# Low parts of w_out and w_in formed on GpSimd, with a new order of all steps, in an attention, SoLU and mixture-of-experts kernel

## The chip, the core and the metric

One NeuronCore of one Trainium2 chip runs the whole program. The metric is the device time of one execution in microseconds (us). Work is spread by hand over five engines: PE (TensorE, matmuls and transposes), DVE (VectorE), ACT (ScalarE), POOL (GpSimd) and SP (SyncE, which here issues most of the loads). Each engine carries out its own list of instructions strictly in order.

## The reference

Three layers, one after the other, on 4 batches of 768 tokens (3072 tokens of 320 values, 8 heads of 40):

```
# 1. gated linear attention, per batch and head, over time t
m_new = max(f[t] + m, i[t]);  f_stab = exp(f[t] + m - m_new);  i_stab = exp(i[t] - m_new)
C = f_stab * C + i_stab * v k^T;  n = f_stab * n + i_stab * k
y[t] = sigmoid(o_gate[t]) * (C q) / max(|n q|, 1)
# 2. SoLU layer: w_in is 320 x 1024, w_out is 1024 x 320
h = x @ w_in;  solu = h * softmax(h)
out = (layernorm(solu) * g_ln) @ w_out
# 3. experts: 8 of them, w1 320 x 1024, w2 1024 x 320, each token goes to one
logits = cosine(x, expert_emb) / tau;  e = argmax(logits)
out = softmax(logits)[e] * (relu(x @ w1[e]) @ w2[e])
```

## The kernel before

**Precision.** PE multiplies in a reduced format (fp32r). So that the result stays accurate, every large matrix is kept as a high part (the value cast to fp32r) and a low part (value minus high part, again fp32r), and a product is a sum of three: high by high, low by high, high by low. For w_in the parts are WH and WL, for w_out OH and OL.

**Attention.** The tokens are cut into 24 groups of 128, six per batch, handled side by side for the four batches' chunks. For each group there are the loads `load_q` (512 KB) and `load_n` (484 KB, keys, values and output gate), the scores S (PE, L626) weighted into Pt (DVE, L631), the values scaled by the gates (`scale_v`, POOL, L615; called vprep below), the numerator (PE, L637 and L642), the state (L647), and the denominator and gate (DVE, L654 to L662), which give X. X is transposed and split into xh and xl.

**SoLU layer.** `hidden` (L686 to L690) computes half of H = x @ w_in in one PSUM tile, and `hidden_pair` (L694, L695) ends it. There is one H tile: mm1 of group g+1 cannot begin before group g's H has been read for the last time. DVE takes the row maximum (L699, negmax), ACT the exponential (L704), DVE multiplies (L709, umul, the last reader of H). Then u is transposed, split, and multiplied with OH and OL (L748 to L750).

**Experts.** A routing stage runs every four or six groups (L783 to L845): POOL makes one-hot matrices ohr (L837) and ohv (L839), four pairs each time, which PE multiplies (L845, called invm). After the 24 groups, tokens are gathered per expert by indirect DMA (POOL, L1118), transposed on PE (L1129, xt), multiplied with the expert's weights, and scattered (L1222).

**The weights at the start.** w_in and w_out come as 64-bit floats. Each part is loaded by SP into a staging buffer `raw` (four slots, two per load, so a third load of this kind waits for the decode of the first), and DVE turns it into 32-bit values by three integer instructions (`decode`, L397 to L399; called dec_in0 to dec_in3 and dec_out0, dec_out1; the second and third instruction read two operands from SBUF). ACT casts the high parts (w_in: L421, called whi; w_out: L566, ohi). DVE forms the low parts: w_in by `in_lo` (L428, a subtract; called wlo(0) to wlo(3), 128x512 each) and w_out by `out_lo` (L569, one scale-and-subtract instruction; olo(0) to olo(7), 128x320 each). Half 0 of mm1 reads wlo(0) and wlo(2), half 1 reads wlo(1) and wlo(3). PE transposes w_out (L525, wtr), to fold the expert embedding in (L538, L546), and sums OH and OL over rows with eight matmul pairs (L576, cm).

**The gates.** A chain of its own: gate loads, a scan (L348), six matmuls (L356), a second scan (L358, gsum), twelve matmuls (L365), an exponential on ACT (L367, gives gw). vprep of the first group needs gw.

**What sets the order.** A table AT gives every step a number. The steps are sorted by it, and each engine's list is what results. The `after` and `war` arguments of `add` are used to make sure that the order is a legal one; waits in the program come from the data that an instruction reads and writes.

Of the kernel before, what the change touches and what calls it, by code (L numbers as in the profile page):

```python
# [9 lines left out]
F32 = mybir.dt.float32  # L10
# [48 lines left out]
BUFS = {"raw": 4, "qk": 4, "nat": 4, "Pt": 2, "X": 1, "xh": 2, "xl": 2, "e": 1, "u": 2, "ut": 1, "xg": 5, "yo": 3, "og": 1}  # L59
NFILL = 10  # L60
INP = ((0, 1), (1, 2), (2, 4), (4, 5))
# [157 lines left out]
def moe_kernel(ctx: ExitStack, tc: tile.TileContext, qkT, nat, gates, w_in, w_out, emb, w1, w2, cst, out):  # L219
# [59 lines left out]
    wts = {}  # L279
# [1290 lines left out]
```

## Time and profile before

| what | us |
|---|---|
| time, median of 3 runs | 524.79 (520.2 to 525.45) |
| the profiled execution's time | 522.23 |
| its span, first to last instruction | 520.4 |
| PE busy | 494.0 (95%) |
| DVE busy | 340.0 (65%) |
| ACT busy | 275.0 (53%) |
| POOL busy | 203.9 (39%) |

The profiled execution is one run; its own time is 2.6 us below the median. PE's share of busy time is an average: it is low in the first 48 us and at the end, and close to 100% in between. Times in the rows further below are us from the span's start.

### The profile page before, as it was taken

How to read it: one execution, taken by the hardware profiler on the slowest of the kernel's cores; microseconds unless marked ns; L12 is line 12 of the kernel's file. 1: busy time of each engine (PE TensorE's matmuls, PEld its weight loads, DVE VectorE, ACT ScalarE, POOL GpSimd, SP SyncE). 2: the span in 40 equal slices, each digit the busy share in tenths (PEclk: the TensorE clock that was granted, in tenths of full speed). 3: DMA queues.
4: the chain of work that ended last, by engine and by line, in shares of the span. 5: the costliest groups of instructions: out<-in, count | busy, mean ns of one | idle time of the engine just before them, and what ended most of it. 6: DMA issues, size and time to landing. Idle time of an engine off the chain costs nothing. (4 is left out here: it accounts for less than half of the span.)

```text
span 520.4 us, 14487 instructions
## 1 busy us (share of the span) xinstructions
PE 494.0 (95%) x5925; PEld 452.2 (87%) x5925; DVE 340.0 (65%) x735; ACT 275.0 (53%) x604; POOL 203.9 (39%) x350
## 2 busy tenths in 40 slices
PE   6869999999999999999999899999999999999991
PEld 5747998888899999889898789898999999999991
DVE  5997667777677587677778778677463655485120
ACT  3572555665656556666467565554543644565220
POOL 3221223266246247345315683656172444112021
PEclk9989999999999999999999899999999999999996
DMA  8962233343341253414041412835631861563000
GB/s 300 412 223 81 80 83 120 113 147 111 90 144 46 77 156 121 144 40 143 3 171 44 152 47 96 276 84 193 231 92 44 285 223 64 217 189 121 14 21 31
DMA packets 20139, 68.01 MB, mean 131 GB/s; under 512 B 2658, under 2 KB 6050, under 8 KB 19680
## 3 DMA queue, kind: packets, MB, share of 16 engines
q1 hardware_dynamic: 17120, 58.27, 33.5%
q0 software_dynamic: 2944, 8.73, 5.3%
q8 instruction: 49, 0.80, 0.7%
q14 instruction: 26, 0.21, 0.1%
HBM read 58.31 MB, written 8.72 MB: 129 GB/s over the span
## 5 line engine op out<-in xcount | busy, mean ns | idle before, releaser
L1222 POOL DMA_INDIRECT out_x<-you,sidx x28 | 30.8, 1099 | 95.5 <-ACT you L1215 82.9
L748 PE MATMUL Y<-OH,uh 128*128 128x328 f32 x192 | 63.4, 330 | 0.0
L1190 DVE SCALAR_TENSOR_TENSOR lu<-hpu,uu 128x384 fp32r<-128x384 f32 (+4 forms) x56 | 28.6, 519 | 53.0 <-ACT uu L1184 43.5
L750 PE MATMUL Y<-OH,ul 128*128 128x328 f32 x192 | 60.3, 314 | 0.2 <-DVE ul L740 0.2
L749 PE MATMUL Y<-OL,uh 128*128 128x328 f32 x192 | 60.4, 315 | 0.0
L1208 PE MATMUL ypu<-hr,uu 128*128 128x320 f32 (+4 forms) x192 | 60.1, 313 | 0.0
L1209 PE MATMUL ypu<-lr,uu 128*128 128x320 f32 (+4 forms) x192 | 59.3, 309 | 0.0
L1184 ACT ACTIVATE uu<-hpu 128x384 fp32r<-128x384 f32 (+7 forms) x64 | 30.4, 483 | 52.2 <-PE hpu L1161 40.0
L1109 DVE TENSOR_TENSOR lr<-raw,hr 128x1024 fp32r<-128x1024 f32 (+1 forms) x32 | 43.4, 1355 | 15.1 <-ACT hr L1102 15.1
L1210 PE MATMUL ypu<-hr,lu 128*128 128x320 f32 (+4 forms) x168 | 51.8, 309 | 0.0
L1102 ACT CAST hr<-raw 128x1024 fp32r<-128x1024 f32 (+1 forms) x40 | 45.2, 1134 | 10.5 <-DMA raw<-in_w 9.4
L736 ACT CAST uh<-tpu 128x512 fp32r<-128x512 f32 x48 | 27.7, 586 | 38.7 <-PE tpu L732 38.4
L704 ACT ACTIVATE e<-H,nmx 128x1024 f32<-128x1024 f32 x24 | 26.8, 1117 | 40.2 <-DVE nmx L699 40.2
L1118 POOL DMA_INDIRECT xgr<-ys,gidx x28 | 36.5, 1302 | 27.3 <-issue 8.9
L699 DVE TENSOR_REDUCE nmx<-H 128x1 f32<-128x1024 f32 x24 | 29.4, 1224 | 26.1 <-PE H L695 24.5
L1157 PE MATMUL hpu<-exr,hr 128*128 128x384 f32 (+7 forms) x128 | 43.7, 341 | 0.0
L1158 PE MATMUL hpu<-exr,lr 128*128 128x384 f32 (+7 forms) x128 | 42.5, 332 | 0.0
L1159 PE MATMUL hpu<-exr,hr 128*128 128x384 f32 (+7 forms) x128 | 42.4, 332 | 0.0
L686 PE MATMUL H<-WH,xh 128*128 128x512 f32 x96 | 40.7, 424 | 1.2 <-DVE u L709 1.1
L740 DVE TENSOR_TENSOR ul<-tpu,uh 128x512 fp32r<-128x512 f32 x48 | 32.4, 687 | 12.6 <-ACT uh L736 12.5
L687 PE MATMUL H<-WL,xh 128*128 128x512 f32 x96 | 37.9, 395 | 0.1
L748 PEld LDWEIGHTS Y<-OH,uh 128*128 128x128 f32 x192 | 36.2, 189 | 2.0 <-ACT yr L766 0.2
(230 smaller groups left out, 1351.3 us busy)
## 6 DMA issues: line engine op xcount, KB each, us to landing
qk<-in_qkT SPq DMA_DIRECT2D x24, 512.0 KB, 4.2
raw<-in_w SPq DMA_DIRECT2D x24, 512.0 KB, 4.7
nat<-in_nat SPq DMA_DIRECT2D x24, 484.0 KB, 3.7
raw<-in_w SPq DMA_DIRECT2D x16, 640.0 KB, 5.3
ys<-yr SPq DMA_DIRECT2D x5, 772.0 KB, 5.0
raw<-in_w_out SPq DMA_DIRECT2D x2, 1280.0 KB, 9.3
raw<-in_w_in SPq DMA_DIRECT2D x3, 512.0 KB, 6.4
raw<-in_w_in SPq DMA_DIRECT2D x1, 1024.0 KB, 8.3
```

Source lines behind the costliest of these rows:

```text
L686: T.matmul(out=o, lhsT=xh[:, kk, :], rhs=WH[:, kk, f], start=(kk == 0), stop=False)
L748: T.matmul(out=yp, lhsT=uh, rhs=OH[:, k, :], start=(k == 0), stop=False)
L749: T.matmul(out=yp, lhsT=uh, rhs=OL[:, k, :], start=False, stop=False)
L750: T.matmul(out=yp, lhsT=ul, rhs=OH[:, k, :], start=False, stop=(k == 7))
L1102: A.copy(out=R.h[i], in_=R.raw[i])
L1109: eng.tensor_tensor(out=R.l[i], in0=R.raw[i], in1=R.h[i].bitcast(F32), op=ALU.subtract)
L1157: T.matmul(out=o, lhsT=R.h[k][:, fs_], rhs=xh[:, k, tk], start=(k == 0), stop=False)
L1158: T.matmul(out=o, lhsT=R.l[k][:, fs_], rhs=xh[:, k, tk], start=False, stop=False)
L1159: T.matmul(out=o, lhsT=R.h[k][:, fs_], rhs=xl[:, k, tk], start=False, stop=False)
L1208: T.matmul(out=yp, lhsT=uh, rhs=hi, start=(f == 0), stop=False)
L1209: T.matmul(out=yp, lhsT=uh, rhs=lo, start=False, stop=False)
L1210: T.matmul(out=yp, lhsT=ul, rhs=hi, start=False, stop=(f == 7))
```

## The change

Four things change.

- The four low parts of w_in (wlo) are formed by POOL instead of DVE, with the same subtract.
- The eight low parts of w_out (olo) are formed by POOL. POOL's instruction is a plain subtract, so the scaling by g_ln is a new ACT instruction, `out_sc` (128x320, in place), one for each part; as it overwrites w_out's values, it stands behind the transposes wtr of the same part.
- The table AT has new numbers throughout. The loads and steps of the opening stand in another order, and so do steps on all engines later.
- PACE names, for eight expert weight loads, an earlier step that they are ordered behind.

```diff
+OLO_G, WLO_G, DEC_G = range(8), range(4), ()
+PACE = {(r, i): [("xc", u, 3)] for u, w in ((1, ((3, 1), (2, 3), (2, 2), (2, 1))), (3, ((3, 0), (4, 3), (3, 3), (3, 2)))) for r, i in w}
 AT = {
-    "f_in": "546 70 429 10",
+    "f_in": "498 167 373 2",
...
-            add(("wlo", j), "V", lambda j=j: in_lo(j, V), after=[("whi", j)])
+            add(("wlo", j), "G" if j in WLO_G else "V", lambda j=j: in_lo(j, G if j in WLO_G else V), after=[("whi", j)])
...
+    def out_sc(k):
+        A.mul(wts["o", k // 4][:, k % 4], wts["o", k // 4][:, k % 4], gl[:, k:k + 1])
+
     def out_lo(k):
-        V.scalar_tensor_tensor(out=wts["OL"][:, k, MAIN], in0=wts["o", k // 4][:, k % 4], scalar=gl[:, k:k + 1], in1=wts["OH"].bitcast(F32)[:, k, MAIN], op0=ALU.mult, op1=ALU.subtract)
+        if k in OLO_G:
+            G.tensor_tensor(out=wts["OL"][:, k, MAIN], in0=wts["o", k // 4][:, k % 4], in1=wts["OH"].bitcast(F32)[:, k, MAIN], op=ALU.subtract)
...
+        if k in OLO_G:
+            add(("osc", k), "A", lambda k=k: out_sc(k), after=[("ohi", k), ("wtr", k)])
+        add(("olo", k), "G" if k in OLO_G else "V", lambda k=k: out_lo(k), after=[("osc" if k in OLO_G else "ohi", k)])
...
-                add(("wl", r, i), "S", lambda r=r, R=R, i=i: w_load(R, od["ev", r], i), after=[("ev", r)], war=[("dec_out", 1)], take="raw", size=.512 * wsize(i))
+                add(("wl", r, i), "S", lambda r=r, R=R, i=i: w_load(R, od["ev", r], i), after=[("ev", r)] + PACE.get((r, i), []), war=[("dec_out", 1)], take="raw", size=.512 * wsize(i))
```

Line numbers after the change are 3 to 13 higher (L399 becomes L402, L428 becomes L431, L569 becomes L576 for POOL, L615 becomes L626, L699 becomes L710).

**First place: SP's first loads.** In the kernel before, SP's list begins with the constants cs and one part of w_in. raw is a load of w_in or w_out, 128x2560 is half of w_out.

```order
L313 DMA cs<-in_cst 128x329
L392 DMA raw<-in_w_in 128x1024
L312 DMA gx<-in_gates 32x768
L605 DMA qk_154<-in_qkT 128x1024
L311 DMA gt<-in_gates 32x1536
L612 DMA nat_158<-in_nat 128x968
L315 DMA cmb<-in_emb 8x320
L392 DMA raw<-in_w_in 128x1024
L605 DMA qk_169<-in_qkT 128x1024
L605 DMA qk_179<-in_qkT 128x1024
L392 DMA raw<-in_w_out 128x2560
```

The same place after the change, from the start of SP's list to the second part of w_in:

```order
L395 DMA raw<-in_w_in 128x1024
L395 DMA raw<-in_w_out 128x2560
L316 DMA cs<-in_cst 128x329
L623 DMA nat_154<-in_nat 128x968
L314 DMA gt<-in_gates 32x1536
L616 DMA qk_162<-in_qkT 128x1024
L623 DMA nat_164<-in_nat 128x968
L315 DMA gx<-in_gates 32x768
L318 DMA cmb<-in_emb 8x320
L395 DMA raw<-in_w_in 128x1024
```

Half of w_out moved from eleventh to second, and the constants and both gate loads (gt, gx) stand behind it.

**Second place: DVE from the last decodes to the first negmax.** Before, with wf a part of w_in, of a half of w_out, nmx the result of negmax(0):

```order
L399 SCALAR_TENSOR_TENSOR wf_210<-raw,wf_210 128x512
L428 TENSOR_TENSOR WL<-wf_511,WH 128x512
L428 TENSOR_TENSOR WL<-wf_210,WH 128x512
L428 TENSOR_TENSOR WL<-wf_511,WH 128x512
L560 TENSOR_TENSOR oe<-tpz,cs 128x64
L569 SCALAR_TENSOR_TENSOR OL<-of_256,cs,OH 128x320
L569 SCALAR_TENSOR_TENSOR OL<-of_386,cs,OH 128x320
L679 TENSOR_TENSOR xl_585<-tpx_558,xh_568 128x384
...
L569 SCALAR_TENSOR_TENSOR OL<-of_256,cs,OH 128x320
L569 SCALAR_TENSOR_TENSOR OL<-of_386,cs,OH 128x320
L699 TENSOR_REDUCE nmx_679<-H_161 128x1
```

After, on DVE, from X of the first group (X_362) to the last decode:

```order
L673 SCALAR_TENSOR_TENSOR X_362<-num_308,og_360 128x320
L642 TENSOR_TENSOR Pt_390<-S_1_342,cs 128x512
L642 TENSOR_TENSOR Pt_390<-S_1_343,cs 128x512
L400 TENSOR_SCALAR wf_416<-raw 128x1024
L401 SCALAR_TENSOR_TENSOR wf_416<-raw,wf_416 128x1024
L402 SCALAR_TENSOR_TENSOR wf_416<-raw,wf_416 128x1024
L400 TENSOR_SCALAR wf_213<-raw 128x512
L401 SCALAR_TENSOR_TENSOR wf_213<-raw,wf_213 128x512
L402 SCALAR_TENSOR_TENSOR wf_213<-raw,wf_213 128x512
```

The low parts are gone from DVE's list, and no decode of w_out is left behind X of the first group. And on POOL after the change, from its first low part to the last (nat is vprep; before, POOL's list holds only the rows of nat here):

```order
L431 TENSOR_TENSOR WL<-wf_213,WH 128x512
L576 TENSOR_TENSOR OL<-of_168,OH 128x320 x3
L626 TENSOR_TENSOR nat_154<-nat_154,gw 128x328
L626 TENSOR_TENSOR nat_184<-nat_184,gw 128x328
L576 TENSOR_TENSOR OL<-of_168,OH 128x320
L626 TENSOR_TENSOR nat_187<-nat_187,gw 128x328
L626 TENSOR_TENSOR nat_164<-nat_164,gw 128x328
L576 TENSOR_TENSOR OL<-of_266,OH 128x320 x2
L626 TENSOR_TENSOR nat_405<-nat_405,gw 128x328
L431 TENSOR_TENSOR WL<-wf_416,WH 128x512
L431 TENSOR_TENSOR WL<-wf_213,WH 128x512
L431 TENSOR_TENSOR WL<-wf_416,WH 128x512
```

Four low parts (wlo(1) and three olo) stand ahead of the first group's vprep, nat_154, and wlo(2), wlo(0), wlo(3) stand behind the fifth vprep.

**Third place: POOL at the fifth routing stage.** Before, with nmx21 the statistics of group 21 and ohr4, ohv4 the one-hot pairs:

```order
L715 TENSOR_SCALAR nmx21_4618<-nmx21_4618 128x1
L837 TENSOR_SCALAR ohr4_0_4693<-cs_75,vr4_4684 128x128
L839 TENSOR_SCALAR ohv4_0_4695<-cs_75,vr4_4684 128x192
L837 TENSOR_SCALAR ohr4_1_4723<-cs_75,vr4_4684 128x128
L839 TENSOR_SCALAR ohv4_1_4725<-cs_75,vr4_4684 128x192
```

And after:

```order
L848 TENSOR_SCALAR ohr4_2_4682<-cs_75,vr4_4663 128x128
L850 TENSOR_SCALAR ohv4_2_4684<-cs_75,vr4_4663 128x192
L848 TENSOR_SCALAR ohr4_3_4699<-cs_75,vr4_4663 128x128
L850 TENSOR_SCALAR ohv4_3_4701<-cs_75,vr4_4663 128x192
L724 TENSOR_SCALAR nmx21_4631<-nmx21_4631 128x1
```

Two of the four pairs moved ahead of the statistics of group 21. On DVE the key that they need (vr4) moved likewise, from behind umul(21) to ahead of the gating of group 23 and umul(21). PE's product of the pairs stands at the same place in both, between the two halves of mm2(21).

## Rows read from the trace of the kernel before

**Rows 1.** Waits of PE, whole span: what for, us in total, times, longest.
```profile
PE txr L1129 <- DMA xgr<-ys,gidx: 2.2, 3, 1.1
PE ip L845 <- POOL ohv L839: 1.9, 1, 1.9
PE H L686 <- DVE u L709: 1.1, 1, 1.1
```

**Rows 2.** Windows: us, busy PE PEld DVE ACT POOL, clock, DMA share, GB/s.
```profile
0.00:5.00 5.00, 1.83 (x8) 1.83 (x9) 1.68 (x5) 1.89 (x3) 3.10 (x17) 1.00 0.65 187
5.00:10.00 5.00, 4.07 (x32) 3.37 (x30) 2.99 (x4) 1.43 (x3) 0.00 (x0) 1.00 1.00 338
10.00:15.00 5.00, 4.85 (x28) 3.12 (x28) 4.39 (x9) 1.80 (x5) 0.83 (x2) 1.00 1.03 423
```

**Rows 3.** Timeline of PE, opening: start us, us, instruction, [idle before, releaser].
```profile
9.50 1.02 PE L356 MATMUL H<-gt,cs 128*128 128x512 f32 x2
...
38.45 0.48 PE L686 MATMUL H<-WH,xh 128*128 128x512 f32 x1
...
42.23 0.49 PE L694 MATMUL H<-WH,xl 64*128 64x512 f32 x1
...
48.10 0.47 PE L686 MATMUL H<-WH,xh 128*128 128x512 f32 x1 [1.06 <-DVE u L709]
```

**Rows 4.** Timeline of DVE, opening; columns as in the group before.
```profile
14.40 1.75 DVE L358 TENSOR_TENSOR_SCAN gx<-H,z 32x767 f32<-32x767 f32 x1 [0.48 <-PE H L600]
...
17.39 0.82 DVE L397 TENSOR_SCALAR of<-raw 128x1280 int32<-128x1280 int32 x1
...
19.77 1.91 DVE L399 SCALAR_TENSOR_TENSOR of<-raw,of 128x1280 int32<-128x1280 int32 x1
...
23.75 1.28 DVE L631 TENSOR_TENSOR Pt<-S,cs 128x512 f32<-128x512 f32 x2
...
31.50 1.17 DVE L397 TENSOR_SCALAR wf<-raw 128x1024 int32<-128x1024 int32 x1
...
35.38 0.43 DVE L397 TENSOR_SCALAR wf<-raw 128x512 int32<-128x512 int32 x1 [0.19 <-DMA raw<-in_w_in]
...
37.18 2.43 DVE L428 TENSOR_TENSOR WL<-wf,WH 128x512 fp32r<-128x512 f32 x3
...
39.67 1.00 DVE L569 SCALAR_TENSOR_TENSOR OL<-of,cs,OH 128x320 fp32r<-128x320 f32 x2
...
43.31 1.01 DVE L569 SCALAR_TENSOR_TENSOR OL<-of,cs,OH 128x320 fp32r<-128x320 f32 x2
44.23 1.22 DVE L699 TENSOR_REDUCE nmx<-H 128x1 f32<-128x1024 f32 x1
...
46.73 1.22 DVE L709 SCALAR_TENSOR_TENSOR u<-e,H 128x1024 f32<-128x1024 f32 x1 [0.16 <-ACT e L704]
```

**Rows 5.** Timeline of POOL, opening, the scaling of the values (vprep).
```profile
19.27 3.70 POOL L615 TENSOR_TENSOR nat<-nat,gw 128x328 f32<-128x328 f32 x3 [7.53 <-ACT gw L367]
27.63 1.78 POOL L615 TENSOR_TENSOR nat<-nat,gw 128x328 f32<-128x328 f32 x1 [4.67 <-DMA nat<-in_nat]
31.38 0.74 POOL L615 TENSOR_TENSOR nat<-nat,gw 128x328 f32<-128x328 f32 x1 [1.97 <-DMA nat<-in_nat]
```

**Rows 6.** POOL's instructions with fp32r output: ns min/median/max, first and last start.
```profile
L837 POOL TENSOR_SCALAR ohr<-cs,vr x22: 593/622/1622, 114.7 to 312.3; 128x128 fp32r<-128x128 f32 x22
L839 POOL TENSOR_SCALAR ohv<-cs,vr x22: 993/1002/1018, 115.3 to 312.9; 128x192 fp32r<-128x192 f32 x22
```

**Rows 7.** Timeline of POOL and PE, fifth routing stage: the last pair, PE's wait.
```profile
291.13 1.00 POOL L839 TENSOR_SCALAR ohv<-cs,vr 128x192 fp32r<-128x192 f32 x1
...
292.18 0.47 PE L845 MATMUL ip<-ohv,ohr 128*128 128x192 f32 x2 [1.89 <-POOL ohv L839]
```

**Rows 8.** Window behind that wait; columns as in the windows above.
```profile
294.00:296.00 2.00, 2.00 (x10) 1.95 (x9) 0.75 (x3) 0.00 (x0) 0.67 (x2) 0.50 0.48 195
```

**Rows 9.** Timeline of PE, the longest wait for a gather.
```profile
331.46 0.81 PE L1129 MATMUL txr<-cs,xgr 112*128 112x112 f32 x6 [1.12 <-DMA xgr<-ys,gidx]
```

More of the change, by code (lines that the diff above doesn't have):

```diff
@@ L392, in fetch_w, with decode @@
         SY.dma_start(out=raws[name], in_=src.bitcast(I32))
-    def decode(name, d):
+    def decode(name, d, V=V):
         r = raws.pop(name).rearrange("p (f b) -> p f b", b=2)
@@ L415, in in_decode @@
             wts["f", k] = tl("sg", [P, DF if k < 2 else 512], f"wf{k}")
-        decode(f"wi{p}", wts["f", k].bitcast(I32)[:, f.start:f.start + 512 * (b - a)])
+        decode(f"wi{p}", wts["f", k].bitcast(I32)[:, f.start:f.start + 512 * (b - a)], G if p in DEC_G else V)
     def in_hi(j):
@@ L566, in out_hi @@
         A.mul(wts["OH"][:, k, MAIN], wts["o", k // 4][:, k % 4], gl[:, k:k + 1])
+    def out_sc(k):
+        A.mul(wts["o", k // 4][:, k % 4], wts["o", k // 4][:, k % 4], gl[:, k:k + 1])
     def out_lo(k):
-        V.scalar_tensor_tensor(out=wts["OL"][:, k, MAIN], in0=wts["o", k // 4][:, k % 4], scalar=gl[:, k:k + 1], in1=wts["OH"].bitcast(F32)[:, k, MAIN], op0=ALU.mult, op1=ALU.subtract)
+        if k in OLO_G:
+            G.tensor_tensor(out=wts["OL"][:, k, MAIN], in0=wts["o", k // 4][:, k % 4], in1=wts["OH"].bitcast(F32)[:, k, MAIN], op=ALU.subtract)
+        else:
+            V.scalar_tensor_tensor(out=wts["OL"][:, k, MAIN], in0=wts["o", k // 4][:, k % 4], scalar=gl[:, k:k + 1], in1=wts["OH"].bitcast(F32)[:, k, MAIN], op0=ALU.mult, op1=ALU.subtract)
     def out_mean(k):
@@ L584, in moe_kernel @@
         add(("ohi", k), "A", lambda k=k: out_hi(k), after=[("dec_out", k // 4)])
-        add(("olo", k), "V", lambda k=k: out_lo(k), after=[("ohi", k)])
+        if k in OLO_G:
+            add(("osc", k), "A", lambda k=k: out_sc(k), after=[("ohi", k), ("wtr", k)])
+        add(("olo", k), "G" if k in OLO_G else "V", lambda k=k: out_lo(k), after=[("osc" if k in OLO_G else "ohi", k)])
         add(("cm", k), "P", lambda k=k: out_mean(k), after=[("olo", k), "eohi", "eolo", "onefr"] + ([("cm", k - 1)] if k else []), take=() if k else "Y")
@@ L1355, in redo @@
                     out_hi(k)
+                    if k in OLO_G:
+                        out_sc(k)
                     out_lo(k)
```

249 rows, old and new, of the table AT are left out of this document.

## The prediction, made before the changed kernel was run

> **What bounds the kernel now.** I read the list of PE's waits first. PE is busy 494.0 of the span's 520.4 us, so some 26 us is all that any order can give back, and the waits that carry a name are short: 1.9 us at the fifth routing stage, 2.2 us in three waits for gathers, 1.1 us for umul [rows 1]. The rest lies in the opening, so I read that as windows and as timelines of each engine. After 48 us PE runs with almost no gap; whatever makes PE's stream of SoLU matmuls start earlier therefore moves everything behind it, unless a new wait takes it back. That stream really starts with mm1 of group 1 at 48.10 [rows 3]. What ends last in front of it is a chain: DVE decodes the last part of w_in at 35.38 to 37.18, mm1(0) starts at 38.45, its last matmul pair at 42.23 ends near 42.6, and then negmax does not start: DVE forms low parts from 37.18 on, the last from 43.31, and negmax begins at 44.23, 1.6 us after H was ready. Exponential and umul (46.73, 1.22 us) follow, and 48.10 comes right behind umul [rows 3, 4]. The decode itself waited only 0.19 us for its load; DVE, not the transfer, was late. So the opening is bound by DVE, and the change takes work from DVE there.
>
> **The gates' chain is later.** In the new list of SP the first load of w_out (1280 KB) stands ahead of the constants and the gates. Up to and with the smaller gate load gx, the last that the six gate matmuls need, 512 + 1280 + 164 + 484 + 192 + 512 + 484 + 96 = 3724 KB are ahead (sizes from the shapes in the list, at 4 bytes). The three 5-us windows moved 0.94, 1.69 and 2.12 MB [rows 2], so 3.8 MB are through at about 12.6 us. The gate matmuls began at 9.50 [rows 3] and gsum 4.9 us later at 14.40 [rows 4]; from 12.4 on that gives 17.2, and the first vprep, 4.87 us behind gsum's start (19.27, rows 4 and 5), comes at about 22.0 instead of 19.27. X of the first group, done at 23.8 before, is done at about 25.5: 2.7 us later, less about 1 us since vprep and the gating had been stretched (19.27: three in 3.70 us, where one alone takes 0.74) [rows 5].
>
> **The decodes are earlier all the same.** Behind X, DVE before had 13.4 us until 37.18. After, the list shows only Pt (1.28), the big decode of w_in (31.50 to 35.19, 3.7) and the last (1.8) [rows 4]: 6.8 us, so the last decode ends at 25.5 + 6.8 = 32.3. The second decode of w_out (4.3 us, as 17.39 to 21.68 [rows 4]) now fills DVE's wait for the gates. The load of that last part has 996 KB less ahead of it, about 2.4 us at the third window's rate, so it will not be what is late. mm1(0) started 1.3 us behind the last decode [rows 3, 4]; PE now has transposes, embedding matmuls and a group's scores in front of it that stood elsewhere, for which I add about a microsecond: mm1(0) at about 34.7 instead of 38.45.
>
> **The low parts.** DVE loses 12 instructions: four subtracts (2.43 for three) and eight of about 0.5 [rows 4]. ACT gains eight scalings of 128x320; nearest is DVE's own pass at 0.5 us, so 4 us, spread over the opening between other work that waits for transposes; ACT is busy 1.4 to 1.9 us of each of the first three windows of 5 [rows 2], and I cost it at nothing (0 to 1 us if it delays the last casts of w_in).
>
> What POOL takes for a subtract with fp32r output no row shows. From below: vprep alone, 0.74 us for 328 columns [rows 5], gives 1.15 us for 512 and 0.72 for 320. From above: the one-hot instructions, 1.00 us for 192 columns and at the median 0.62 for 128 [rows 6], give 2.7 and 1.7; their worst, 1.62 for 128, gives 6.5 and 4.1. The operation is that of vprep, the output type that of the one-hots; I take 1.8 and 1.1. Where does it lie? POOL's list puts wlo(1) and three olo ahead of the first vprep. wlo(1) can start at about 16 (its decode follows the scan at 13 to 15.5), the three olo at about 18.4, since the scaling waits for the transposes behind the gate matmuls: 18.4 + 3 x 1.1 = 21.7, just ahead of 22.0. At 2.7 the vprep is 1.9 us late. Behind, wlo(2) and wlo(0) run from about 31 and 32.9: done at 34.7, when mm1(0) wants them, at 36.4 with the upper price.
>
> A row shows a collision that counts here: vprep at 27.63 took 1.78 us instead of 0.74 [rows 5], while DVE's third decode instruction ran (27.33 to 28.82). 27.63 + 1.78 is 0.59 behind that instruction's end: as if it had stood still until then. The Trainium skill has this as a rule (SBUF — State Buffer, section on its two separate sides): a DVE instruction with two SBUF operands and a GpSimd instruction that reads SBUF exclude each other, and whoever starts first holds the ports for its whole length. The trace agrees. By that rule moving the low parts to GpSimd beside DVE's decodes speaks against this change; an estimate by it is one or two holds of up to 1.5 us, so a gain in the opening of about 2 instead of 3.7.
>
> **The sum for the opening.** mm1(0) 34.7, its H complete 4.1 us later at 38.8, negmax without the old 1.6 us, and umul's end 3.7 us behind negmax's start as before (44.23 to 47.95 [rows 4]) gives 42.6; PE fills that time with group 2's attention, five short matmul steps and now half of the transposes of u (about 0.5 us, that stood behind), so mm1 of group 1 at 43.5 to 46 instead of 48.10. I take a gain of 3.5 us, bounds 2 to 4.5 as long as POOL's price is not above 2.7.
>
> **Behind the opening.** At the fifth routing stage POOL's four pairs ended at 292.13 and PE waited 1.89 us [rows 7]. In the new list the key on DVE comes ahead of a gating and a umul (about 2.2 us earlier) and two pairs ahead of the statistics, while PE's product stands where it was. Behind the wait PE ran at clock 0.50 for over two windows [rows 8], half of its upper level of 2.4 GHz; that too goes if the wait goes. Bounds 0 and 1.9 + 1.7; I take 1.5. The longest wait for a gather, 1.12 us [rows 9], has twelve more matmuls ahead of it now: 0 to 1.1, I take 0.7. Against it stands that the whole order is new on every engine; the kernel before shows 4 to 5 us of waits after 48 us, most of it in the first two of [rows 1], and the new order will have its own elsewhere: -1 to +4, I take +1. PACE I cost at nothing: the list of the changed kernel shows the loads it names in another order, and no wait of theirs on POOL or PE for the named steps; their waits are the same kinds as before.
>
> Sum: -3.5 - 1.5 - 0.7 + 1.0 = -4.7 against the profiled execution's 522.23, thus 517.5; against the median of 524.79 it would be 520.1. I say 519.
>
> **The rivals.** *A, the forecast*: 517 to 522, chance 0.45. *B, all of it comes*: opening 4.5, routing stage with its slow windows 3.6, gather 1.1, no new waits: 9 less, about 513 to 516. For it: each has its row; against it: three good ends at once. Chance 0.20. *C, given back*: mm1 starts 2 to 4 us earlier but the collision with the decodes and new waits in the rest take it back; 522 to 527. For it: PE needs its 494 us in any order, and every reshuffle that removed one wait can make another, as the routing stages have only a microsecond or two to spare. Chance 0.20. *D, slower*: POOL's subtract is dear. POOL is in order, so the first vprep waits for one wlo and three olo, and DVE's last decodes wait behind X, which waits for that vprep. At 3.5 us for 512 columns (2.2 for 320) the vprep starts at 16 + 3.5 + 6.6 = 26, 4 us late, and the gain is gone; this is the point that decides. At the one-hots' worst rate, 6.5 and 4.1, it starts at 16 + 6.5 + 12.3 = 35, 13 us late, and the time is 524.8 + 13 - 7, about 531. For it: that rate occurs with fp32r output; against it: only as a maximum while DVE was busy. Chance 0.15.
>
> **How the numbers follow.** One per cent, 5.2 us, is about what a measurement of this kernel can tell from no change. A straddles that line below the median: of its 0.45 I count 0.25 as faster and 0.20 as same. B is faster (0.20), C same but for 0.02, D slower. Faster 0.45, same 0.38, slower 0.17. The range leaves out the lower part of B and D: 513 to 526. The likeliest one's own range is 516 to 522.
>
> **What would show it.** Right: negmax(0) on DVE straight behind the last matmul of mm1(0); mm1 of group 1 at 43.5 to 46; POOL's subtract of 512 columns at 1.1 to 2.7 us; the wait at the fifth invm under a microsecond and no window at clock 0.50 behind it. Wrong: the first vprep later than 24, the last decode ending later than 35, a clock of 0.50 during the gate matmuls (constants, and with them PE's first matmul, come some 4 us later than now), or an idle time of PE after 48 us that is above the present 5.

## The result, and the profile after

The changed kernel took 518.97 us in the median of 12 runs (518.44 to 521.64), the kernel before 525.59 in 12 runs beside it (520.2 to 525.92). The medians differ by 6.6 us. The ratio on record, by which the experiments below are compared too, is 0.9898 with a 95% interval of 0.9874 to 0.9923, or 5.4 us. The change is faster by about 1%: the sign is clear of noise, but the interval lies on both sides of the 1% at which the prediction draws its line. The profiled execution took 519.02 us with a span of 517.3, against 522.23 and 520.4 before, so those two differ by 3.2 us only. Where the other 3.4 us of the medians come from is a large part of what follows.

First the waits of PE after the change (what for: us in total, times, longest), beside [rows 1]:

```profile
PE H L611 <- DMA cs<-in_cst: 8.4, 1, 8.4
PE H L611 <- DVE gx L361: 1.5, 1, 1.5
PE ip L856 <- POOL ohv L850: 1.3, 1, 1.3
...
PE num L648 <- POOL nat L626: 0.9, 1, 0.9
PE txr L1140 <- DMA xgr<-ys,gidx: 0.8, 2, 0.5
```

PE no longer idles for umul ahead of mm1 of group 1, its wait at the routing stage went from 1.9 to 1.3, those for gathers from 2.2 to 0.8, and its first instruction now waits 8.4 us for the constants. The timeline of PE (start us, us, instruction), the opening and the routing stage, beside [rows 3] and [rows 7]:

```profile
8.35 1.23 PE L611 MATMUL H<-cs 128*128 128x128 f32 x4 [8.35 <-DMA cs<-in_cst]
...
13.12 1.84 PE L637 MATMUL S<-qk 40*128 40x128 f32 x16
14.89 1.12 PE L359 MATMUL H<-gt,cs 128*128 128x512 f32 x2
...
18.43 0.59 PE L359 MATMUL H<-gx,negi 128*128 128x256 f32 x2
...
22.94 1.45 PE L368 MATMUL gx<-cs,gx 128*128 128x64 f32 x12
...
39.88 0.48 PE L697 MATMUL H<-WH,xh 128*128 128x512 f32 x1
...
43.30 0.50 PE L705 MATMUL H<-WH,xl 64*128 64x512 f32 x1
...
48.30 0.48 PE L697 MATMUL H<-WH,xh 128*128 128x512 f32 x1
...
291.35 0.58 PE L856 MATMUL ip<-ohv,ohr 128*128 128x192 f32 x3 [1.33 <-POOL ohv L850]
```

The gate matmuls begin at 14.89 instead of 9.50, mm1(0) at 39.88 instead of 38.45, mm1 of group 1 at 48.30 instead of 48.10. By this pair of profiles the opening gained nothing. DVE, beside [rows 4]: the second decode of w_in, which waits for its load, gsum, a stretched decode of w_out, X of the first group, two instructions of the last decode, negmax(0) and umul(0).

```profile
15.44 0.43 DVE L400 TENSOR_SCALAR wf<-raw 128x512 int32<-128x512 int32 x1 [1.70 <-DMA raw<-in_w_in]
...
19.36 1.75 DVE L361 TENSOR_TENSOR_SCAN gx<-H,z 32x767 f32<-32x767 f32 x1
...
22.10 2.04 DVE L401 SCALAR_TENSOR_TENSOR of<-raw,of 128x1280 int32<-128x1280 int32 x1
...
29.40 0.49 DVE L673 SCALAR_TENSOR_TENSOR X<-num,og 128x320 f32<-128x320 f32 x1
...
34.12 1.09 DVE L400 TENSOR_SCALAR wf<-raw 128x512 int32<-128x512 int32 x1
...
36.39 1.66 DVE L402 SCALAR_TENSOR_TENSOR wf<-raw,wf 128x512 int32<-128x512 int32 x1
...
43.84 1.23 DVE L710 TENSOR_REDUCE nmx<-H 128x1 f32<-128x1024 f32 x1 [0.75 <-PE H L706]
...
46.59 1.17 DVE L720 SCALAR_TENSOR_TENSOR u<-e,H 128x1024 f32<-128x1024 f32 x1
```

negmax now waits for H and for nothing else. POOL, beside [rows 5]: the first wlo, three olo, the first two vpreps, a single olo.

```profile
18.06 1.27 POOL L431 TENSOR_TENSOR WL<-wf,WH 128x512 fp32r<-128x512 f32 x1 [0.63 <-ACT WH L424]
20.52 4.34 POOL L576 TENSOR_TENSOR OL<-of,OH 128x320 fp32r<-128x320 f32 x3 [1.20 <-ACT of L572]
24.99 2.50 POOL L626 TENSOR_TENSOR nat<-nat,gw 128x328 f32<-128x328 f32 x2
27.46 0.86 POOL L576 TENSOR_TENSOR OL<-of,OH 128x320 fp32r<-128x320 f32 x1
```

This is the price that no row of before showed: 1.27 us for 512 columns and 0.86 for 320 while DVE runs no decode, and 1.45 each, on average, for the three beside DVE's decode of w_out. At the routing stage the wait is 1.33 us, and the window behind it, beside [rows 8] and with its columns, is at full clock:

```profile
294.00:296.00 2.00, 1.95 (x14) 1.57 (x12) 1.86 (x10) 1.73 (x6) 0.00 (x0) 1.00 0.37 152
```

### The profile page after: what moved, and what is told of

It reads as the page before. It is cut to its first block, busy times and chain, and to the rows that moved or that the text cites. A ratio compares the mean times of both kernels' runs of the same rounds, so it can differ in the third digit from the quotient of the medians.

```text
span 517.3 us, 14495 instructions
## 1 busy us (share of the span) xinstructions
PE 490.9 (95%) x5925; PEld 449.9 (87%) x5925; DVE 338.2 (65%) x723; ACT 278.4 (54%) x612; POOL 213.0 (41%) x362
## 5 line engine op out<-in xcount | busy, mean ns | idle before, releaser
L710 DVE TENSOR_REDUCE nmx<-H 128x1 f32<-128x1024 f32 x24 | 29.4, 1223 | 31.0 <-PE H L706 29.7
L1129 POOL DMA_INDIRECT xgr<-ys,gidx x28 | 29.2, 1042 | 39.0 <-issue 16.1
L1168 PE MATMUL hpu<-exr,hr 128*128 128x384 f32 (+7 forms) x128 | 43.5, 340 | 0.1
```

The source lines that it names most:

```text
L1168: T.matmul(out=o, lhsT=R.h[k][:, fs_], rhs=xh[:, k, tk], start=(k == 0), stop=False)
```

## The experiments

The comparisons with the kernel before were made anew in each group of runs (medians 526.12, 525.96, 525.63 and 525.33), so the ratios are what to compare. "mm1(1)" is the start of mm1 of group 1, "last" the start of the last matmul, and "between" their difference, all in the one profiled execution of each. `MOVE` gives the steps that it names new numbers in AT.

| kernel | median us | ratio to before, 95% | mm1(1) | last | between |
|---|---|---|---|---|---|
| before (first profile) | 525.59 | 1 | 48.10 | 509.45 | 461.35 |
| changed | 518.97 | 0.9898 (0.9874 to 0.9923) | 48.30 | 506.06 | 457.76 |
| e1 before again | 525.60 | 0.9986 (0.9957 to 1.0015) | 51.88 | 512.51 | 460.63 |
| e2 low parts on DVE, new order | 520.31 | 0.9893 (0.9838 to 0.9948) | 50.07 | 508.13 | 458.06 |
| e3 before's opening, new rest | 522.01 | 0.9931 (0.9901 to 0.9961) | 52.14 | 510.87 | 458.73 |
| e4 new opening, before's rest | 522.51 | 0.9953 (0.9923 to 0.9983) | 48.20 | 508.62 | 460.42 |
| e5 before, two fills moved | 522.45 | 0.9931 (0.9895 to 0.9967) | 48.51 | 508.36 | 459.85 |
| e6 low parts on POOL, old order | 526.62 | 1.0011 (0.9977 to 1.0045) | 50.89 | 514.54 | 463.65 |
| e7 routing stage undone | 521.52 | 0.9905 (0.9872 to 0.9939) | 48.95 | 508.92 | 459.97 |
| e8 constants first | 521.73 | 0.9936 (0.9906 to 0.9966) | 49.38 | 506.49 | 457.11 |
| e9 changed again | 519.82 | 0.9896 (0.9869 to 0.9923) | 48.72 | 507.13 | 458.41 |
| e10 two fills, new rest | 519.88 | 0.9891 (0.9863 to 0.9919) | 49.53 | 507.71 | 458.18 |
| e11 gates' chain freed | 519.84 | 0.9903 (0.9871 to 0.9935) | 48.14 | 506.29 | 458.15 |
| e12 new mix | 519.32 | 0.9889 (0.9867 to 0.9911) | 48.17 | 505.59 | 457.42 |

**e1: the kernel before, once more.**

> The kernel before, unchanged, to see how its own executions spread and what clock each has. Its profiled execution took 522.23 us at a mean clock of 0.985 while the median is near 525.6. Theory: the slower executions hold one more stretch of PE at half clock, so time and mean clock go together, about 520 at 0.99 and 525.5 at 0.975. Rival: the spread has another cause and the clock is the same in all.

Its runs went from 522.65 to 526.59, and this profiled execution took 524.92 us. Its opening is not that of the first profile. The first scores in the first profile of the kernel before, then PE's timeline in e1:

```profile
7.86 1.16 PE L626 MATMUL S<-qk 40*128 40x128 f32 x16 [0.93 <-DMA qk<-in_qkT]
```

```profile
3.12 3.78 PE L600 MATMUL H<-cs 128*128 128x128 f32 x16 [3.12 <-DMA cs<-in_cst]
8.26 2.08 PE L626 MATMUL S<-qk 40*128 40x128 f32 x16 [1.35 <-DMA qk<-in_qkT]
...
11.28 1.92 PE L356 MATMUL H<-gt,cs 128*128 128x512 f32 x2
...
41.65 0.69 PE L546 MATMUL tpz<-cs,ept 128*128 128x128 f32 x2 [3.01 <-ACT ept L541]
41.99 0.78 PE L686 MATMUL H<-WH,xh 128*128 128x512 f32 x1
...
47.23 0.49 PE L694 MATMUL H<-WH,xl 64*128 64x512 f32 x1
```

Two windows of the same profile (us, busy PE PEld DVE ACT POOL, clock, DMA share, GB/s):

```profile
12.00:14.00 2.00, 2.00 (x4) 0.83 (x3) 1.93 (x5) 0.00 (x0) 0.14 (x1) 1.00 1.09 447
42.00:44.00 2.00, 2.00 (x7) 1.50 (x6) 2.00 (x6) 0.24 (x1) 0.00 (x0) 0.50 0.00 0
```

The first scores take 2.08 us where they took 1.16 in the first profile, the first gate matmuls 1.92 where they took 1.02 [rows 3]. So PE ran at about half rate there, although the windows of that time show a granted clock of 1.00: the column does not show PE's slow start. The Trainium skill (TensorE: Matmul & The Clock Gate, Part 1) says that PE starts out throttled and that sustained work releases it; the durations agree. What differs ahead of it is that PE idled 1.35 us for the first load of q and k, and 0.93 in the first profile. The profiles of e3 and e6, which have the same steps up to there, are like e1: idle times of 1.21 and 1.30 us, and 2.08 us for the scores. In e1 gsum thereby comes at 17.72 instead of 14.40 [rows 4]. At the end of the opening PE idles 3.01 us and then does mm1(0) at clock 0.50, the lower of its two levels; mm1 of group 1 starts at 51.88 instead of 48.10. DVE, X of the first group, the last decode, the last low parts and negmax(0):

```profile
26.67 0.49 DVE L662 SCALAR_TENSOR_TENSOR X<-num,og 128x320 f32<-128x320 f32 x1
...
39.98 0.69 DVE L399 SCALAR_TENSOR_TENSOR wf<-raw,wf 128x512 int32<-128x512 int32 x1
...
46.72 1.01 DVE L569 SCALAR_TENSOR_TENSOR OL<-of,cs,OH 128x320 fp32r<-128x320 f32 x2
47.77 1.22 DVE L699 TENSOR_REDUCE nmx<-H 128x1 f32<-128x1024 f32 x1
```

Here H and DVE's low parts are ready at the same time: the last matmuls of mm1(0) end at 47.72, the last low part at 47.73, and negmax starts at 47.77.

So the execution from which the prediction was worked out was a quick one: three of the four profiles that begin with these steps have the slow start. On the clock the theory of the expectation failed: mean clock and time do not go together (526.2 us at 0.990, 522.65 at 0.988), which fits a slow start that the column leaves out.

**e2: the new order, the low parts back on DVE.**

```diff
-OLO_G, WLO_G, DEC_G = range(8), range(4), ()
+OLO_G, WLO_G, DEC_G = (), (), ()
```

> The changed kernel with its new order, but the low parts of w_in and w_out formed by DVE again (no scaling by ACT). By the prediction's own reasons DVE bounds the opening, so 12 instructions more on it (6.3 us) cost 3 to 5 us: 522 to 524. By the trace of the changed kernel, where DVE's decodes were stretched by 3.1 us in sum while POOL formed low parts and DVE stood idle for 1.6 us ahead of the first den, the cost is 0 to 2 us: 519 to 521.

0.9893, the ratio of the changed kernel itself, as the second half of the expectation had it. On top of the new order, moving the low parts to POOL shows no gain; with four runs the interval leaves room for some 3 us either way. From X to the end of the last decode DVE took 7.6 us here (31.68 to 39.27), with two low parts between, and 8.2 us in the changed kernel (29.89 to 38.05), with none: there the three instructions of the last decode took 1.09, 1.11 and 1.66 us instead of 0.41, 0.69 and 0.69, stretched by POOL's work. What DVE saves there on low parts it spends on stretched decodes. (mm1 of group 1 is 1.8 us later in this profile because the fills and the twelve gate matmuls behind gsum ran at half rate, the latter in 2.66 us instead of 1.45.)

**e3 and e4: the two halves of the order.** e3 numbers every step up to mm1 of group 1 as before (low parts on DVE) and all others as after; e4 the other way round, and without PACE.

> All steps up to mm1 of group 1 in the order of before, with the low parts on DVE as before; everything behind in the new order. If the gain lies behind the opening (the routing stage with its half-clock stretch, and the gathers), this is as fast as the changed kernel: 518.5 to 520.5. If the opening carries it, as the prediction had it (3.5 of 4.7 us), this keeps only a quarter: 522 to 525.

> The counterpart: all steps up to mm1 of group 1 in the new order, with the low parts on POOL and the scaling on ACT; everything behind in the order of before. If the gain lies behind the opening: 523 to 526, no faster than before, with the wait of about 1.9 us for the one-hot pairs at the fifth routing stage and the stretch at clock 0.50 behind it. If the opening carries it: 520 to 522.

0.9931 and 0.9953: neither part carries the gain alone. e3's 522.01 lies at the edge of the range that left the new rest a quarter, and e4's 522.51 lies between its two ranges. 3.6 and 2.5 us, each give or take 1.6, add up to 6.1; the whole change gave 5.4 by its ratio and 6.6 by the medians. The table shows the same in two places: e4 begins mm1 of group 1 as early as the changed kernel (48.20) and then takes as long as before (460.42), e3 begins as late as e1 (52.14) and is then quick (458.73).

**e5: two fills in the kernel before.** A fill is a step of two dummy matmuls (four rows in a timeline).

```diff
+MOVE = {('fill', 4): 117, ('fill', 5): 118}
...
+        at.update({k: n for k, n in MOVE.items() if k in at})
```

> The kernel before with two of its ten fill steps (dummy matmuls of PE, four rows each) moved ahead of the first scores, where PE idled 1.35 us in a typical execution and ran on at half its rate until 14.7 us, while in the execution profiled first it idled 0.93 us and ran at full rate from 7.86. Theory: the idle time is what leaves PE slow; with the gap filled the first scores take 1.16 us instead of 2.08, the gate matmuls come up to 3 us earlier, and the median falls to 522 to 523.5. Rival: PE is slow for a while whatever it does, or the lateness is made up by the loads: 525 to 526.5.

0.9931 with two dummy steps in another place, as its theory had it. PE's timeline:

```profile
3.11 5.16 PE L604 MATMUL H<-cs 128*128 128x128 f32 x24 [3.11 <-DMA cs<-in_cst]
8.20 1.16 PE L630 MATMUL S<-qk 40*128 40x128 f32 x16
9.39 1.10 PE L360 MATMUL H<-gt,cs 128*128 128x512 f32 x2
```

PE works through, and the first scores and gate matmuls are at full rate. gsum came at 14.42, as in the first profile. e10 and e12, which have the same two fills early, also show the scores near full rate (1.33 and 1.16 us). So moving two fills takes the slow start away, and by the ratio that gives 3.6 us. Whether the closed gap does it or the additional work ahead of the scores, no run separates. That the median, 522.45, is near the time of the first profile is in part chance, since that profile also holds the half-clock stretch at the routing stage.

**e6: the low parts on POOL, the old order.** The table of before, with the eight scalings just ahead of the olo.

> The other half of the change alone: the order of before on every engine, but the twelve low parts on POOL, with the eight scalings on ACT just ahead of them. By the prediction DVE bounds the opening and negmax(0) waits 1.6 us behind low parts: 1.5 to 2.5 us faster, 523 to 524. By the typical execution of before, where the first H is ready only when DVE is already done with the low parts, and PE waits for the last decode and not for low parts: 0 to 1 us, 525 to 526.

1.0011: no gain is measured, and the interval leaves room for one of 1.2 us. DVE (negmax waits for H) and PE (mm1(0) waits for a low part on POOL), from its profile:

```profile
46.77 1.22 DVE L710 TENSOR_REDUCE nmx<-H 128x1 f32<-128x1024 f32 x1 [2.45 <-PE H L706]
```

```profile
43.04 0.49 PE L698 MATMUL H<-WL,xh 128*128 128x512 f32 x1 [0.33 <-POOL WL L431]
```

DVE idles 2.45 us ahead of negmax: without the low parts it waits for H, which in e1 came just when DVE was done with them. mm1 of group 1 is 1.0 us earlier than in e1; the median does not show it. (The rest of this profiled execution holds a wait of 1.5 us for a gather and a stretch at clock 0.50 behind it, which is no part of the edit.)

**e7: the fifth routing stage undone.** `MOVE = {('key', 4): 5562, ('okr', 4, 2): 5700, ('okr', 4, 3): 5701}` in the changed kernel.

> The changed kernel with one thing undone: the key of the fifth routing stage on DVE behind umul(21) again, and its four one-hot pairs on POOL all behind the statistics of group 21. The wait of PE for the pairs should go back from 1.33 to about 1.9 us. If that is all: 519.5, 0.6 us slower than the changed kernel. If the longer wait also brings back a stretch at clock 0.50 behind it in most executions: 521 to 522.

Its profile shows the wait, now in two pieces, and the stretch at half clock:

```profile
PE ip L860 <- POOL ohv L854: 2.4, 2, 1.2
```

```profile
296.00:298.00 2.00, 2.00 (x11) 1.95 (x10) 1.26 (x7) 0.51 (x1) 0.18 (x1) 0.50 0.00 0
```

That execution needs 459.97 us from mm1(1) to the last matmul, 2.2 more than the changed kernel. The median, 521.52, lies in the second range of the expectation, but the ratio, 0.9905, is within the interval of the changed kernel's, so this does not settle how often the stretch comes.

**e8: constants first.** `MOVE` puts the load of the constants first on SP and six fills ahead of wd (the low part of w_in's last columns, formed on PE).

> The changed kernel with the constants (164 KB) as SP's first load and six of the ten fill steps ahead of the low part of w_in's last columns, so that PE starts at about 3.1 instead of 8.35 us and spends its slow start on fills. If the gates' chain, late because PE was slow until 14.9 us, still holds up the opening, gsum comes at 17 to 18 instead of 19.4, and mm1 of group 1 1 to 2.5 us earlier: 516.5 to 518. If the loads hold it up, or the fills taken from ahead of the twelve gate matmuls leave PE idle and slow there: 519 to 520.5.

0.9936, slower than the changed kernel's 0.9898 but not clearly so; the median lies above both ranges of the expectation. The last of the six gate matmuls and gsum:

```profile
16.92 0.59 PE L363 MATMUL H<-gx,negi 128*128 128x256 f32 x2
```

```profile
19.18 1.75 DVE L365 TENSOR_TENSOR_SCAN gx<-H,z 32x767 f32<-32x767 f32 x1
```

The gate matmuls ended 1.5 us earlier than in the changed kernel (17.51 instead of 19.02), and gsum came as late as ever: it starts without an idle time of DVE, right behind the second decode of w_in, Pt and two small steps, and that decode waited for its load until 15.26. Freeing PE did not help, since DVE's list and that load held gsum. The twelve gate matmuls moved up to 21.18, and then the wait moved on:

```profile
PE num L652 <- POOL nat L630: 3.4, 1, 3.4
PE gx L372 <- ACT wt L538: 2.1, 1, 2.1
```

The first vprep stands behind four low parts on POOL and starts at 24.64, 1.4 us after ACT was done with gw (23.26). PE waits 3.4 us for it and runs from 24 to about 34 us at clock 0.50. Here the order on POOL holds the chain up, as rival D had it, though not by the price of a subtract.

**e9 and e10: the changed kernel again, and fills with the new rest.** e10 is e3 with the two fills of e5; no work is moved to POOL.

> The changed kernel, unchanged, on the chip of the two below, as their reference and to see its spread: about 519 to 520.5 here, with a mean clock near 0.99 in most executions and a few executions 2 to 3 us longer at 0.985.

> Before's opening (low parts on DVE) with two fill steps ahead of the first scores, and the changed kernel's order behind mm1 of group 1. If the two effects found so far add up (fills 3.5 us, new rest about 3 us), 519 to 520: as fast as the changed kernel without any work moved to POOL. If they are two ways to the same gain: 521.5 to 523.

0.9896 and 0.9891. Two fills and the new rest give all that the change gives, within what these runs can tell. In e10 PE waits 2.5 us for the embedding and does mm1(0) at half clock:

```profile
PE tpz L553 <- ACT ept L548: 2.5, 1, 2.5
```

```profile
40.00:42.00 2.00, 2.00 (x6) 1.53 (x6) 2.00 (x6) 0.25 (x1) 0.00 (x0) 0.50 0.00 0
```

**e11: the gates' chain freed.** In the changed kernel, `MOVE = {('fill', 1): 412.2, ('fill', 2): 412.4, ('fill', 3): 412.6, ('olo', 3): 474, ('olo', 1): 475, ('olo', 7): 743}`.

> The changed kernel with its gates' chain freed: three fill steps, which waited for gsum and stood 1.8 us long ahead of the twelve gate matmuls, go behind them; on POOL two of the three low parts of w_out ahead of the first vprep go behind the second one, and one that collided with the last decodes goes to the end. If this chain is what holds up the opening (first vprep at 25.0, X done at 29.9), mm1 of group 1 comes 1 to 2 us earlier: 517 to 518.5 against 519 to 520 for the changed kernel. If loads or the decodes themselves do, or PE falls to half rate for want of fills: no gain, or 1 to 2 us slower.

0.9903, no gain; the span of its profile, 517.3 us, is that of the changed kernel. The twelve gate matmuls came at 22.04 instead of 22.94, X ended at 29.40 instead of 29.89, the last decode at 37.89 instead of 38.05: what was freed in the chain went into stretched decodes, since POOL's low parts only moved beside other decodes.

**e12: a mix meant to beat both.** Before's opening with two fills early and four late, low parts of w_out on POOL behind the fifth vprep, low parts of w_in on DVE, new rest.

> An attempt at a better version from what the runs showed: the opening in before's order, but two fill steps ahead of the first scores and the last four between the transposes of X and the transposes of the embedding (there PE idled 2.5 us in the kernel with two fills and the new rest, and ran mm1(0) at clock 0.50); low parts of w_out on POOL, all behind the fifth vprep, where DVE decodes little, so that negmax(0) does not wait for them; low parts of w_in on DVE; behind mm1 of group 1 the new order. If PE's slow stretches are the main thing left in the opening: no window at 0.50 there, mm1 of group 1 at 47 to 48.5 and 517 to 519. If the order of the opening matters less than what PE waits for at the end of it (casts and scalings on ACT): 519 to 520.5, no faster than the changed kernel.

0.9889, level with the changed kernel. The half clock was not avoided: PE idled 2.2 us until 30.39, and the windows from 32 to 38 us are at 0.50. PE's timeline shows the late fills in the way:

```profile
37.08 2.75 PE L615 MATMUL H<-cs 128*128 128x128 f32 x16
39.66 0.38 PE L553 MATMUL tpz<-cs,ept 128*128 128x128 f32 x2
39.80 0.48 PE L701 MATMUL H<-WH,xh 128*128 128x512 f32 x1
```

ept, which the embedding's matmuls (tpz) ahead of mm1(0) read, was done on ACT at 37.5, the cast of xh at 37.9 and the low parts of w_in on DVE at 38.5. By these rows mm1(0) could have started over 1 us earlier without the four fills; no run shows it.

## Why the prediction came out

The time (519 forecast, 518.97 measured) lies within the range, and the change was faster, as forecast. That the two agree so closely is luck: 519 was set between two bases, and the amount was -4.7 us forecast, -3.2 between the two profiles and -6.6 between the medians. Of the forecast's signs, negmax straight behind H, the price of a subtract and the full clock behind the fifth routing stage came. Two did not: mm1 of group 1 was to start at 43.5 to 46 and started at 48.30, and PE's wait at that stage was to fall under a microsecond and was 1.33. Of the steps:

- **What bounds the opening.** The chain that was read, last decode, mm1(0), negmax behind low parts, umul, mm1(1), was that of one quick execution. In e1 the slow start puts everything back by some 3.3 us ahead of it (gsum at 17.72 instead of 14.40), mm1(0) runs at half clock, and negmax starts as soon as H is there, not 1.6 us later. DVE is as busy as in the first profile and done with the low parts just when H is ready, so to take work off DVE alone gains little. This step was wrong because one profile was taken for all; the gap between 522.23 and the median of 524.79, and the spread of the three runs, were the sign.
- **The gates' chain.** Forecast 2.7 us later by the loads up to gx (gate matmuls at 12.4, gsum at 17.2, first vprep at 22.0). Measured 14.89, 19.36, 24.99. The gate matmuls did not wait for their loads; PE, which begins at 8.35 with the constants, was slow until about 14.7 (four fp32 matmul steps of wd 1.97 us instead of 1.07), and they ended at 19.02. But gsum, at 19.36, starts without an idle time of DVE. In DVE's list the second decode of w_in stands ahead of it; its load came at 15.44, after 1.70 us of idle time, and the decode, Pt and two small steps filled DVE from there. e8 and e9 show which of the two held gsum: there the gate matmuls ended at 17.51 and 18.28, and gsum came at 19.18 and 19.77, again straight behind DVE's list. The sum stopped counting loads at gx, and put the end of that decode at 15.5 where it came at 17.32. Behind gsum, 1.8 us of fills stood ahead of the twelve gate matmuls. The delay of the constants the sum had counted as nothing; only its last paragraph named it, and both signs given there, a first vprep later than 24 and a last decode later than 35, came. (The loads as summed end at 12.6, not 12.4; that changes nothing here.)
- **The decodes.** From the first vprep to X the forecast had 3.5 us; measured 4.9, as the first two vpreps took 2.50 us beside the end of DVE's decode of w_out. From X to the last decode it had 6.8 us instead of 13.4. Measured 8.2 (29.89 to 38.05), in e1 13.5 (27.16 to 40.67). The order did what was said: the decode of w_out went into DVE's wait for the gates. The other 1.4 us went back through the collision with POOL: the three instructions of the last decode took 3.86 us instead of 1.82. mm1(0) thus started at 39.88 where 34.7 was forecast: 3.0 us from the gates' chain, 1.4 from the vpreps, 1.4 from the decodes, less 0.6 behind them. The forecast had put such collisions at about 1.7 in an estimate by a rule of the Trainium skill. That rule (SBUF — State Buffer, section on its two separate sides) holds here too: DVE's decode of w_out took 2.04 us instead of 1.49 while POOL formed olo. L400, which reads one operand, was stretched as well, 0.43 to 1.09; the section "Who interferes with whom" of the same page of the Trainium skill names tensor_scalar in a two-port mode as another case, and whether L400 runs in one no run here shows.
- **The low parts.** Price forecast 1.8 and 1.1 us; measured 1.27 and 0.86, close to the lower bounds, which came from vprep. But taking them off DVE showed no gain (e2 and e6, within their intervals), where the forecast had it as part of the reason. e10 reaches the same time with all of them on DVE.
- **The sum for the opening.** Forecast 3.5. Against e1: last decode 2.6 earlier, mm1(0) 2.1 earlier and at full clock 1.8 quicker (its last matmuls end 3.9 us after its start, not 5.7), together H 3.9 earlier and mm1(1) 3.6 earlier; e4 gives 2.5 by ratio. Against the profile that was read: -0.2. That the size fits e1 is in part luck: the opening came out later than forecast, and so was the execution to compare it with.
- **Behind the opening.** Forecast 1.2 (1.5 + 0.7 - 1.0). Measured 3.6 by e3's ratio. From mm1(1) to the last matmul it was 459.9 to 461.4 us in four of the five profiles with the old rest (463.7 in e6, with a longer wait for a gather and half clock behind it), and 457.1 to 458.7 with the new one (e7, which undoes a part of it, aside). The routing stage gave 0.56 of wait, and in executions like the first profile some 1.7 us of a stretch at clock 0.50 that did not come; the gathers 1.4, not 0.7. The new waits were 0.4 at 190.68, 0.4 at transposes of gathered tokens, and 0.3 more between the last matmul and the end: the +1 was about right. The term of the routing stage and the gathers was too small.
- **The rivals.** A came, by its time. Of rival B the gather's part came whole and the routing stage's in part; its opening did not, and there were new waits. C's collision was there. D's price did not occur. Its mechanism, vprep behind low parts on POOL, shows in e8 (1.4 us), but hardly in the changed kernel: there ACT was done with gw at 24.92 and vprep started at 24.99. PE's wait of 0.94 us for the first vprep there comes with the vpreps' length beside DVE's decode. PACE costs nothing that these profiles show; it was not run alone.

What stays open: how much of the 3.6 us of the new rest the half-clock stretch at the routing stage carries. PE's wait of 1.9 us there is in all five profiles with the old rest, the stretch behind it in the first one only. But 18 of the 25 runs of the kernel before that stand beside e1 have a mean clock of 0.982 or lower, where e1 has 0.988 and the first profile 0.985, so most executions seem to hold half-clock time that neither profile shows. Nor does any run tell which steps of the new opening's order carry its part.

## What to carry to other kernels

Take more than one profile before working out an opening: if the runs of a kernel spread by several microseconds, the profiled one may not be the one to improve on. Work moved off a busy engine gains only if that engine alone is late, and moved to GpSimd it can come back as longer instructions on VectorE. When a step waits for one engine's result, look also at what stands ahead of it in its own engine's list: here a load that nobody had counted held gsum that way. Two steps of dummy matmuls, moved ahead of the first scores, gave here 0.7%, where the whole re-planned schedule gave 1.0%.

## What the runs showed of the hardware

- PE's first microseconds run at about half rate, in windows whose granted clock reads 1.00. With an idle time of 1.21 to 1.35 us behind 3.78 us of fills it was slow until about 15 us (e1, e3, e6); with 0.93 us in the first profile of before, and with two more fills in e5, it was at full rate in the first scores, from 7.86 and 8.20. In the changed kernel it was slow from 8.35 to about 14.7, in e9 until about 13.
- A stretch at granted clock 0.50 came with or behind idle times of PE of 1.89 (the first profile), 2.5 (e10), 2.67 (e2) and 3.01 us (e1, where the clock fell some 0.4 us into the idle time), and behind two of 1.14 and 1.22 close together (e7). It did not come behind the waits of 1.33 us at the routing stage, and not behind every longer one: the 1.9 us there brought it in the first profile and not in e1, e4, e5 or e6, and 2.10 us in e11 and 2.5 us in e9 did not.
- A subtract of GpSimd with fp32r output costs 1.27 us for 512 columns, 0.86 for 320; the longest, beside DVE's decodes, took 1.73 and 1.97. DVE's decodes beside them grew as well, from 1.49 to 2.04 (L401 on 128x1280) and from 0.43 to 1.09 (L400 on 128x512).
